# Causal scores cut into four blocks of 32 keys on four column strips, and a slab's TensorE work drawn together into one block

## The chip, the cores and the metric

The kernel runs on one core of a Trainium2 chip. The metric is device time in microseconds from the start to the end of one execution; 652.51 us is the median of three executions of the kernel before (652.41, 652.51 and 654.05). TensorE (PE) multiplies matrices; the loading of its stationary operand has its own rows (PEld). VectorE (DVE), ScalarE (ACT) and GpSimd (POOL) work elementwise, and SyncE (SP) issues the DMAs, in order.

## The reference

A gated linear attention over 768 steps for 4 batches of 8 heads of 48, and a feed-forward layer over its 3072 rows:

```python
def _attn_ref(q, k, v, a_re, a_im):
    mag = np.sqrt(a_re * a_re + a_im * a_im)
    scale = np.minimum(mag, 0.999) / (mag + 1e-06)
    a_re_n, a_im_n = a_re * scale, a_im * scale
    for t in range(S):
        ar, ai = a_re_n[:, :, t, :, None], a_im_n[:, :, t, :, None]
        new_re = ar * S_re - ai * S_im
        new_im = ar * S_im + ai * S_re
        kv = np.einsum('bhd,bhe->bhde', k[:, :, t], v[:, :, t])
        S_re, S_im = new_re + kv, new_im
        y[:, :, t] = np.einsum('bhd,bhde->bhe', q[:, :, t], S_re)
...
    g = x @ w_gate                                   # 384 x 1536
    return (g / (1.0 + np.exp(-g)) * (x @ w_val)) @ w_out
```

## The kernel before, in words

The sequence is cut into 6 chunks of 128 steps. A **slab** is one chunk of one batch (24 slabs, 0 to 23; slabs 0 to 3 are the first chunk, c = 0, and slabs 20 to 23 the last, c = 5). Two slabs form a group, and a group's 256 rows go through the feed-forward layer together (12 groups).

For a group, `stage_ops` turns decay and phase into scaled q and k of 96 columns per head (48 real, 48 imaginary; tiles `qs` and `ks`). `slab_ops` transposes them to 96 partitions (tile `T`) and then has TensorE do three things for a slab:

- **scores** (`sc0`, `sc1`, line 628, PSUM tile `p_ps`): for each of the 8 heads one f32 product of 128 keys by 128 queries over 96 rows, four heads in one operation; VectorE multiplies them with the causal mask (`mk0`, `mk1`, line 634, tile `sc`);
- **state and values** (`av`, line 659, tile `p_py`): the outputs lie in 12 blocks of 32 columns on four column strips of the array (partitions 0, 32, 64, 96 of PSUM), and each block adds the old state times q (`p_py<-T,G`, 96 rows, only where c > 0) and the masked scores times v (`p_py<-sc,vt`, 128 rows), in steps of four matmuls, one on each strip;
- **new state** (`kv`, line 686, tile `p_pm`): 24 products of 32 by 48 on three strips (not in the last chunk), which VectorE adds to G (`ga`) and decays (`gm`).

Then ScalarE copies `p_py` to `xh` (`evh`) and VectorE keeps the rest in `xl` (`evl`). `ffn_ops` works on them in 12 steps per group: `f1` (line 839; from group 1 on 18 products of 128 by 256), silu on ScalarE, `h2`, `hh` and `hl` (VectorE or ScalarE), `f2` (line 873; 6 products of 128 by 384). A f32 matmul has two matmul records in the trace, and an operation of this kind takes twice the records that the program shows. `weight_ops` and `split_ops` make the weights from 64-bit words on VectorE in the first part (lines 738 to 746); `range_ops` loads them again later and reduces them on VectorE (`flags<-wo`, line 791) for a check of their range.

The order on every engine is fixed at build time by `Planner.plan`. It takes an operation when its engine is free in the plan, the one with the lowest key among those that are ready; keys come from due times (`ta` of a slab from `anchor`, `key` of a feed-forward step), and each operation has a cost written by hand, such as `{"PE": 0.88}`. Constants at the top (SWITCH, STRETCH, T0, PER, ...) set due times and penalties. At run time every engine takes its instructions in that order, and waits on semaphores where an operand isn't there.

Of the kernel before, what the change touches and what calls it, by code (L numbers as in the profile page):

```python
# [33 lines left out]
SWITCH_KEY = 8.8  # L34
STRETCH = 1.749
AHEAD, YIELD, QUEUED = -15.32, 14.38, 5.384
T0, PER, FT, FT0 = 47.32, 23.02, 3.999, 5.679
LEAD0, LEAD2 = 8.605, 2.123
CONV0, CONVP = 39.06, 28.89
T1 = T0 + 12 * FT0  # L40
CK0, CKP = 167.9, 18.96
# [4 lines left out]
SHY = -9.417  # L46
# [9 lines left out]
class Op:  # L56
    def __init__(self, idx, name, engs, fn, deps, alloc, table, aim, lat, move, port):
        self.port = port
        self.idx, self.name, self.engs, self.fn, self.deps = idx, name, engs, fn, deps
        self.alloc, self.table, self.aim, self.lat, self.move = alloc, table, aim, lat, move  # L60
        self.start = self.end = self.eng = self.load = None


class Planner:
# [5 lines left out]
    def add(self, name, engs, fn, deps=(), alloc=(), use=(), table=None, key=None, lat=0.0, move=0.0,  # L70
# [7 lines left out]
        return name  # L78

# [15 lines left out]
    def plan(self):  # L95
# [9 lines left out]
        loads = []  # L105
        left, order = [op for op in self.ops if not missing[op]], []
        while left:
            ready = {e: [] for e in free}
            for op in left:
                t = max([d.end + HOP for d in op.deps], default=0.0)  # L110
# [84 lines left out]
def quick(ctx, tc, q, k, v, a_re, a_im, w_gate, w_val, w_out, out, count):  # L195
# [12 lines left out]
    mask = tri.bitcast(F32)  # L208
    ident = const.tile([P, P], F32, name="ident")
# [9 lines left out]
    vts = [const.tile([P, H, 64], F32, name=f"vt{i}") for i in range(2)]  # L219
# [34 lines left out]
    slots = dict(qs=1, ks=1, T=2, dec=3, sc=2, sg=2, hh=2, hl=2, ost=2, xh=2, xl=2, vt=2,  # L254
# [3 lines left out]
    PSUMS = ("gv", "po", "ps", "py", "pm")  # L258
# [13 lines left out]
    for t in fixed:  # L272
        slots[t] = 1
    pl = Planner(slots)
# [277 lines left out]
    def slab_ops(n):  # L552
# [61 lines left out]
        def ldv(e):  # L614
            at_["vt", n] = vts[n % 2]
            nc.sync.dma_start(out=vts[n % 2][:, :, 0:D], in_=v[b, c * P:c * P + P])
        pl.add("ldv" + N, {"SP": 0.55}, ldv, deps=[f"ldv{n - 1}"] if n else [], alloc=[("vt", n)], lat=1.4, move=1.09)
# [4 lines left out]

        for qd in range(2):
            def sc(e, qd=qd):
                qT, kT = views()
                ps = new("ps", f"{n}.{qd}").rearrange("p (h t) -> p h t", h=4)
                for hh in range(4):
                    nc.tensor.matmul(out=ps[:, hh, :], lhsT=kT(4 * qd + hh), rhs=qT(4 * qd + hh), start=True, stop=True)  # L628
            pl.add(f"sc{qd}_{n}", {"PE": 0.88}, sc, deps=tdeps + [f"sc0_{n}" if qd else f"sc1_{n - 1}"],
                   alloc=[("ps", f"{n}.{qd}")], use=[("T", n)], key=ta + qd)  # L630

            def mk(e, qd=qd):
                s = new("sc", f"{n}.{qd}")
                nc.vector.tensor_tensor(out=s, in0=at_["ps", f"{n}.{qd}"].rearrange("p (h t) -> p h t", h=4),  # L634
                                        in1=mask.unsqueeze(1).to_broadcast([P, 4, P]), op=ALU.mult)
            pl.add(f"mk{qd}_{n}", {"DVE": 0.6}, mk, deps=[f"sc{qd}_{n}"], alloc=[("sc", f"{n}.{qd}")],
                   use=[("ps", f"{n}.{qd}")])

        def av(e):
            qT, kT = views()  # L640
            py = new("py", n)[:, :DM].rearrange("p (k t) -> p k t", k=KT)
            vf, gf = flat(vts[n % 2]), flat(G[:, b])

            turns = [[] for _ in range(4)]
            for blk in range(12):
                pr, j = divmod(blk, 3)
                slot, kt_ = blk % 4, blk // 4
                o = py[32 * slot:32 * slot + 32, kt_, :]
                heads = ([(2 * pr, 128 * pr)], [(2 * pr, 128 * pr + 32), (2 * pr + 1, 128 * pr + 48)],
                         [(2 * pr + 1, 128 * pr + 80)])[j]  # L650
                mm = []
                for h, col in heads:
                    if c > 0:
                        mm.append((gf[:, col:col + 32], qT(h)))
                    mm.append((vf[:, col:col + 32], at_["sc", f"{n}.{h // 4}"][:, h % 4, :]))
                turns[slot] += [(o, l, r, i == 0, i == len(mm) - 1) for i, (l, r) in enumerate(mm)]
            for step in zip(*turns):
                for slot, (o, l, r, opens, closes) in enumerate(step):
                    nc.tensor.matmul(out=o, lhsT=l, rhs=r, start=opens, stop=closes, tile_position=(0, 32 * slot))  # L659
        pl.add("av" + N, {"PE": 2.2 if c else 1.3}, av, deps=[f"mk0_{n}", f"mk1_{n}", "ldv" + N, f"gm{n - 4}"],  # L660
               alloc=[("py", n)], use=[("sc", f"{n}.0"), ("sc", f"{n}.1"), ("T", n), ("vt", n)], key=ta + 5)

# [6 lines left out]
        pl.add("evh" + N, {"ACT": 0.4}, evh, deps=["av" + N] + ([f"evh{n - 1}"] if half else []),  # L669
# [10 lines left out]
        if c < NCH - 1:  # L680
            def kv(e):
                pk = new("pm", "K" + N)[:96, :HD].rearrange("p (h d) -> p h d", h=H)
                ks, vt = at_["ks", ("ks", g)][:, hs], vts[n % 2]
                for h in range(H):
                    for j in range(3):
                        nc.tensor.matmul(out=pk[32 * j:32 * j + 32, h, :], lhsT=ks[:, h, 32 * j:32 * j + 32],  # L686
# [438 lines left out]
```

## Time and profile before

| | before |
|---|---|
| median of three executions | 652.51 us |
| the profiled execution | 652.97 us |
| its span, first to last instruction | 651.3 us |
| PE busy | 619.1 us (95%) |
| DVE busy | 498.9 us (77%) |
| ACT busy | 397.5 us (61%) |
| POOL busy | 2.9 us |
| mean granted TensorE clock | 0.999 |

Times in the trace run from the start of the span. "Busy" is time in which at least one instruction of the engine ran; matmuls overlap in the pipeline, so that the distance from one start to the next tells more of a matmul's cost than its length does.

### The profile page before, as it was taken

The numbers are of one execution on the slowest core, as the hardware profiler recorded it, in microseconds if no ns is written. First come the engines' busy times: TensorE is split into PE (matmuls) and PEld (weight loads), VectorE is DVE, ScalarE is ACT, GpSimd is POOL, SyncE is SP. The second block draws the span as 40 slices with busy tenths as digits, with TensorE's granted clock in tenths as the row PEclk, the third lists the DMA queues.
The fourth block names the chain that finished last, engine by engine and source line by source line (L and its number), as shares of the span: only waits on it lengthen the run. The fifth ranks groups of instructions, "written<-read, shape, count | busy, mean of one in ns | idle before, by whom it ended". The sixth has DMA issues, their size and how long they took to land.

```text
span 651.3 us, 15505 instructions
## 1 busy us (share of the span) xinstructions
PE 619.1 (95%) x6306; PEld 578.3 (89%) x6306; DVE 498.9 (77%) x923; ACT 397.5 (61%) x654; POOL 2.9 (0%) x9
## 2 busy tenths in 40 slices
PE   2789999899999999999999999999999999999996
PEld 1467778899998999999999999999999999999995
DVE  8899999989877867977967976966966966643332
ACT  7955259876876958747947757967847836211111
POOL 1000000000000000000000000000000000000000
PEclk9999999999999999999999999999999999999999
DMA  7999102224635544654644555554542530320000
GB/s 233 314 279 361 40 26 74 60 88 124 173 99 148 151 123 115 180 118 118 188 111 118 163 131 123 146 127 119 129 105 60 127 90 16 76 51 1 25 1 29
DMA packets 141748, 77.49 MB, mean 119 GB/s; under 512 B 102363, under 2 KB 137437, under 8 KB 141670
## 3 DMA queue, kind: packets, MB, share of 16 engines
q1 hardware_dynamic: 141670, 76.43, 43.6%
q8 instruction: 51, 0.84, 0.6%
q14 instruction: 27, 0.22, 0.1%
HBM read 57.47 MB, written 4.78 MB: 96 GB/s over the span
## 4 chain that ended last, share of the span: by engine, by line
PE 64%; DVE 17%; ACT 7%; DMA 6%; issue 4%; SPq 1%; DVEq 0%; ACTq 0%
PE p_gv L839 33%; PE p_po L873 16%; PE p_py L659 5%; PE p_ps L628 5%; ACT L956 2%; ACT s L360 2%; DVE xl L742 2%; DMA wo<-in_moe_w_val_dram 2%; PE p_pm L686 2%; PE p_pm L455 2%; DMA wo<-in_moe_w_out_dram 1%; DMA re<-in_a_re_dram 1%; DVE sg L850 1%; DVE sc L634 1%; DVE s L305 1%
## 5 line engine op out<-in xcount | busy, mean ns | idle before, releaser
L839 PE MATMUL p_gv<-xh,ww 128*128 128x256 f32 x1596 | 311.3, 292 | 1.9 <-DVE sg L850 1.9
L839 PEld LDWEIGHTS p_gv<-xh,ww 128*128 128x128 f32 x1596 | 257.9, 190 | 10.7 <-DVE sg L850 4.1
L839 PE MATMUL p_gv<-xl,ww 128*128 128x256 f32 x726 | 202.9, 279 | 0.0
L956 ACT ACT_TABLE_LOAD x111 | 142.4, 1283 | 1.9
L839 PEld LDWEIGHTS p_gv<-xl,ww 128*128 128x128 f32 x726 | 136.4, 188 | 0.2 <-issue 0.2
L845 ACT ACTIVATE sg<-p_gv 128x256 f32<-128x256 f32 x144 | 53.7, 382 | 135.0 <-PE p_gv L839 134.2
L873 PE MATMUL p_po<-wo,hh 128*128 128x384 f32 x484 | 126.4, 342 | 0.0
L850 DVE TENSOR_TENSOR sg<-sg,p_gv 128x256 f32<-128x256 f32 x144 | 58.5, 413 | 61.0 <-ACT sg L845 60.9
L873 PEld LDWEIGHTS p_po<-wo,hh 128*128 128x128 f32 x484 | 81.2, 188 | 2.3 <-issue 2.0
L873 PE MATMUL p_po<-wo,hl 128*128 128x384 f32 x242 | 81.5, 337 | 0.0
L305 DVE TENSOR_TENSOR hl<-sg,hh 128x256 fp32r<-128x256 f32 x132 | 54.3, 417 | 6.7 <-ACT hh L309 1.5
L628 PE MATMUL p_ps<-T 96*128 96x128 f32 x384 | 53.2, 279 | 0.2 <-PE p_gv L839 0.2
L628 PEld LDWEIGHTS p_ps<-T 96*128 96x128 f32 x384 | 50.6, 196 | 1.3 <-PE p_gv L839 0.4
L873 PEld LDWEIGHTS p_po<-wo,hl 128*128 128x128 f32 x242 | 45.4, 188 | 0.0
L309 ACT CAST hh<-sg 128x256 fp32r<-128x256 f32 x49 | 19.8, 405 | 35.3 <-DVE sg L850 31.8
L360 ACT ACTIVATE s<-s 128x768 f32<-128x768 f32 x44 | 36.7, 842 | 5.4 <-DVE s L305 5.0
L659 PE MATMUL p_py<-sc,vt 128*32 128x128 f32 x768 | 37.3, 272 | 1.2 <-ACT xh L668 0.7
L791 DVE TENSOR_REDUCE flags<-wo 128x1 f32<-128x384 f32 x36 | 19.7, 547 | 24.2 <-DMA wo<-in_moe_w_val_dram 11.4
L634 DVE TENSOR_TENSOR sc<-p_ps,tri 128x512 f32<-128x512 f32 x48 | 32.7, 680 | 3.1 <-PE p_ps L628 2.7
L659 PE MATMUL p_py<-T,G 96*32 96x128 f32 x640 | 33.5, 280 | 0.0
L796 ACT ACTIVATE wo<-wo 128x384 f32<-128x384 f32 x36 | 20.1, 558 | 12.8 <-DMA wo<-in_moe_w_gate_dram 6.7
L311 DVE CAST hh<-sg 128x256 fp32r<-128x256 f32 x83 | 23.6, 288 | 4.2 <-PE p_po L873 0.4
(134 smaller groups left out, 804.0 us busy)
## 6 DMA issues: line engine op xcount, KB each, us to landing
T<-ww SPq DMA_DIRECT2D x216, 64.0 KB, 2.1
wo<-in_moe_w_out_dram SPq DMA_DIRECT2D x24, 384.0 KB, 6.6
ww<-in_moe_w_gate_dram SPq DMA_DIRECT2D x12, 384.0 KB, 5.2
vt<-in_v_dram SPq DMA_DIRECT2D x24, 192.0 KB, 3.8
ww<-in_moe_w_val_dram SPq DMA_DIRECT2D x12, 384.0 KB, 5.9
out_dram<-ost SPq DMA_DIRECT2D x24, 192.0 KB, 2.1
wo<-in_moe_w_gate_dram SPq DMA_DIRECT2D x12, 384.0 KB, 3.4
wo<-in_moe_w_val_dram SPq DMA_DIRECT2D x12, 384.0 KB, 3.9
```

What stands on the lines that cost most here:

```text
L305: V[e].tensor_tensor(out=out, in0=a, in1=b, op=op)
L311: nc.vector.tensor_copy(out=out, in_=in_)
L360: nc.scalar.activation(out=of(dst), in_=of(source), func=func, scale=scale, **kw)
L628: nc.tensor.matmul(out=ps[:, hh, :], lhsT=kT(4 * qd + hh), rhs=qT(4 * qd + hh), start=True, stop=True)
L634: nc.vector.tensor_tensor(out=s, in0=at_["ps", f"{n}.{qd}"].rearrange("p (h t) -> p h t", h=4), in1=mask.unsqueeze(1).to_broadcast([P, 4, ...
L659: nc.tensor.matmul(out=o, lhsT=l, rhs=r, start=opens, stop=closes, tile_position=(0, 32 * slot))
L796: nc.scalar.activation(out=high(0), in_=high(1), func=AF.Square, accum_out=flags[:, fl_hi + j:fl_hi + j + 1])
L839: nc.tensor.matmul(out=gv[:, i, :], lhsT=l, rhs=r, start=(m == 0), stop=(m == len(mm) - 1))
L845: nc.scalar.activation(out=new("sg", I), in_=at_["gv", I][:, 0:2 * P], func=AF.Silu)
L850: nc.vector.tensor_tensor(out=sg, in0=sg, in1=at_["gv", I][:, 2 * P:4 * P], op=ALU.mult)
L873: nc.tensor.matmul(out=po, lhsT=l[:, cs], rhs=weight("o", f, part), start=f == 0 and j == 0, stop=f == NF - 1 and j == len(products) - 1)
L956: nc.scalar.preload_act_table_set(op.load)
```

## The change: what it does

- A head's scores are no longer one product of 128 keys by 128 queries but four blocks of 32 keys. Block i has only the queries from 32 i on (128, 96, 64 and 32 columns), since earlier queries see none of its keys. Each block stands on one of the four column strips; strip (i + r) mod 4, where r is the head's place, so that every strip gets blocks of all lengths. The helper `strips` writes the matmuls in the order in which their strips come free by column count.
- Keys of a head are thereby rotated by 32 r partitions. The mask becomes a tile `turn` of 128 x 4 x 128, made at the start on GpSimd; v is loaded a second time with the same rotation (`ldr`, seven DMAs for a slab, tile `vr`), and the unrotated v (`ldv`, contiguous now) is left for `kv` alone, and isn't loaded in the last chunk. The score banks and `vr` are set to zero once at the start on VectorE.
- `av` is split into `st` (state times q, 16 matmuls) and `V` (scores times v, 16 matmuls), and `kv` moves ahead of both. For c > 0, `glue` makes the planner keep TensorE for the chain sc, kv, st, V once sc has begun: nothing else comes between. `sc` then waits for all that the chain needs (T, v, rotated v, `ks`, the decayed state, the banks of `p_py` and `p_pm`).
- `mk0` and `mk1` both follow the whole `sc`.
- 15 of the planner's constants have other numbers, so that other operations change places too.

```diff
-        for qd in range(2):
-            def sc(e, qd=qd):
-                qT, kT = views()
-                ps = new("ps", f"{n}.{qd}").rearrange("p (h t) -> p h t", h=4)
-                for hh in range(4):
-                    nc.tensor.matmul(out=ps[:, hh, :], lhsT=kT(4 * qd + hh), rhs=qT(4 * qd + hh), start=True, stop=True)
+        def strips(turns):
+            ends = [0] * 4
+            while any(turns):
+                slot = min((s for s in range(4) if turns[s]), key=lambda s: ends[s])
+                o, l, r, opens, closes = turns[slot].pop(0)
+                ends[slot] += r.shape[-1]
+                nc.tensor.matmul(out=o, lhsT=l, rhs=r, start=opens, stop=closes, tile_position=(0, 32 * slot),
+                                 skip_group_check=True)
+        def sc(e):
+            qT, kT = views()
+            turns = [[] for _ in range(4)]
+            for qd in range(2):
+                for r in range(4):
+                    h = 2 * r + qd
+                    for i in range(4):
+                        slot = (i + r) % 4
+                        turns[slot].append((scores[qd][32 * slot:32 * slot + 32, r, 32 * i:P], kT(h)[:, 32 * i:32 * i + 32],
+                                            qT(h)[:, 32 * i:P], True, True))
+            strips(turns)
...
+        def ldr(e):
+            for r in range(4):
+                for p, t, m in ((32 * r, 0, P - 32 * r), (0, P - 32 * r, 32 * r)):
+                    if m:
+                        nc.sync.dma_start(out=turned_v[n % 2][p:p + m, 2 * r:2 * r + 2, 0:D],
+                                          in_=v[b, c * P + t:c * P + t + m, 2 * r:2 * r + 2])
...
-        pl.add("av" + N, {"PE": 2.2 if c else 1.3}, av, deps=[f"mk0_{n}", f"mk1_{n}", "ldv" + N, f"gm{n - 4}"],
-            pl.add("kv" + N, {"PE": 1.1}, kv, deps=made["ks"] + ["ldv" + N, "av" + N], alloc=[("pm", "K" + N)],
+        link = ["sc" + N]
+        if c < NCH - 1:
+            link.append(pl.add("kv" + N, {"PE": 0.85}, kv, deps=made["ks"] + ["ldv" + N, "sc" + N], alloc=[] if together else kvs,
+        if c > 0:
+            link.append(pl.add("st" + N, {"PE": 0.9}, states, deps=["sc" + N, f"gm{n - 4}"] + ["kv" + N] * (c < NCH - 1),
+        link.append(pl.add("V" + N, {"PE": 1.0 if c else 1.2}, values, deps=[f"mk0_{n}", f"mk1_{n}", "ldr" + N] + ["st" + N] * (c > 0),
+        if together:
+            pl.glue(*link)
...
-        for t in vts:
+        for t in turned_v + scores:
             nc.vector.memset(t, 0.0)
```

The places on TensorE, from slab 8 (c = 2). Before, the scores stand on line 628 in two operations with feed-forward work (`p_gv`, `p_po`) between, and state and values alternate in steps of four on line 659:

```order
L628 MATMUL p_ps<-T 128x128 x4
L873 MATMUL p_po<-wo_929,hh 128x384 x2
...
L628 MATMUL p_ps<-T 128x128 x4
L839 MATMUL p_gv<-xh,ww_918 128x256
...
L659 MATMUL p_py<-T,G 32x128 x4
L659 MATMUL p_py<-sc,vt_79 32x128 x4
L659 MATMUL p_py<-T,G 32x128 x4
...
L873 MATMUL p_po<-wo_959,hh 128x384 x2
...
L686 MATMUL p_pm<-vt_79,ks 32x48 x24
```

After, the same slab is one run of 88 matmuls; the first and the last score blocks are shown (32 in all, of 128, 96, 64 and 32 columns), then new state, state and values:

```order
L656 MATMUL p_ps_90<-T 32x128
L656 MATMUL p_ps_90<-T 32x96
L656 MATMUL p_ps_90<-T 32x64
L656 MATMUL p_ps_90<-T 32x32
...
L656 MATMUL p_ps_91<-T 32x32
L716 MATMUL p_pm<-vt_72,ks 32x48 x24
L656 MATMUL p_py<-T,G 32x128 x16
L656 MATMUL p_py<-sc,vr_74 32x128 x16
L933 MATMUL p_po<-wo_1141,hh 128x384 x2
```

`kv` now stands between the scores and the rest, and no feed-forward work is left between the scores and the values that wait for `mk0` and `mk1`.

On VectorE, the same slab. Before, the two masks (`sc<-p_ps,tri`) stand with another operation between them:

```order
L599 STREAM_TRANSPOSE ww_1400<-ks 128x4x2x3x32
L599 STREAM_TRANSPOSE ww_1400<-qs 128x4x2x3x32
L634 TENSOR_TENSOR sc<-p_ps,tri 128x512
L424 SCALAR_TENSOR_TENSOR s_2413<-s_2413,s_2302 128x768
L634 TENSOR_TENSOR sc<-p_ps,tri 128x512
```

After, they stand one behind the other in every slab, here right behind a reduction of weights that come by DMA (`flags<-wo`) and behind products of the feed-forward steps (`sg`, `hh`, `hl`):

```order
L910 TENSOR_TENSOR sg<-sg,p_gv 128x256 x2
L324 CAST hh<-sg 128x256 x2
L318 TENSOR_TENSOR hl<-sg,hh 128x256 x2
L851 TENSOR_REDUCE flags<-wo_1472 128x1
L679 TENSOR_TENSOR sc<-p_ps_90,turn 128x512
L679 TENSOR_TENSOR sc<-p_ps_91,turn 128x512
L910 TENSOR_TENSOR sg<-sg,p_gv 128x256
L318 TENSOR_TENSOR G<-G,p_pm 96x8x48
```

What stands ahead of the masks differs from slab to slab.

## Rows read from the trace of the kernel before

**Rows 1.** The page: span, busy time of engines, and the first line of the chain that ended last.

```profile
span 651.3 us, 15505 instructions
PE 619.1 (95%) x6306; PEld 578.3 (89%) x6306; DVE 498.9 (77%) x923; ACT 397.5 (61%) x654; POOL 2.9 (0%) x9
...
PE 64%; DVE 17%; ACT 7%; DMA 6%; issue 4%; SPq 1%; DVEq 0%; ACTq 0%
```

**Rows 2.** Busy time by stretch: from and to, length, then busy us (and instructions) of PE, PEld, DVE, ACT, POOL, the granted clock, the DMA engines' share and GB/s.

```profile
30.00:60.00 30.00, 27.15 (x293) 22.41 (x291) 30.00 (x50) 18.80 (x28) 0.00 (x0) 1.00 1.02 308
60.00:90.00 30.00, 30.00 (x212) 23.91 (x211) 30.00 (x54) 8.79 (x16) 0.00 (x0) 1.00 0.26 87
90.00:105.00 15.00, 13.71 (x133) 10.19 (x132) 15.00 (x27) 11.99 (x16) 0.00 (x0) 1.00 0.16 40
105.00:130.00 25.00, 23.24 (x169) 21.48 (x168) 24.72 (x48) 21.85 (x36) 0.00 (x0) 1.00 0.28 79
130.00:160.00 30.00, 29.95 (x369) 28.74 (x370) 27.24 (x44) 21.35 (x34) 0.00 (x0) 1.00 0.37 105
160.00:600.00 440.00, 435.81 (x4773) 420.20 (x4773) 330.10 (x621) 283.53 (x468) 0.00 (x0) 1.00 0.46 116
600.00:640.00 40.00, 40.00 (x304) 40.00 (x303) 14.75 (x39) 5.78 (x15) 0.00 (x0) 1.00 0.03 11
```

**Rows 3.** Timeline of PE around state, values and new state of one slab: start, length of the merged piece, what, and how many records.

```profile
287.63 0.28 PE L839 MATMUL p_gv<-xh,ww 128*128 128x256 f32 x1
287.83 0.43 PE L659 MATMUL p_py<-T,G 96*32 96x128 f32 x8
288.09 0.40 PE L659 MATMUL p_py<-sc,vt 128*32 128x128 f32 x8
288.31 0.41 PE L659 MATMUL p_py<-T,G 96*32 96x128 f32 x8
...
289.45 0.40 PE L659 MATMUL p_py<-sc,vt 128*32 128x128 f32 x8
289.78 0.62 PE L873 MATMUL p_po<-wo,hh 128*128 128x384 f32 x2
290.24 0.34 PE L873 MATMUL p_po<-wo,hl 128*128 128x384 f32 x1
290.42 0.51 PE L873 MATMUL p_po<-wo,hh 128*128 128x384 f32 x2
290.76 0.34 PE L873 MATMUL p_po<-wo,hl 128*128 128x384 f32 x1
291.03 0.88 PE L686 MATMUL p_pm<-vt,ks 128*32 128x48 f32 x48
291.84 0.38 PE L839 MATMUL p_gv<-xh,ww 128*128 128x256 f32 x1
292.06 0.28 PE L839 MATMUL p_gv<-xl,ww 128*128 128x256 f32 x1
292.18 0.40 PE L839 MATMUL p_gv<-xh,ww 128*128 128x256 f32 x2
```

**Rows 4.** Timeline of PE around the scores, from three slabs, and one place (35.19) where the values waited for the mask.

```profile
35.19 0.85 PE L659 MATMUL p_py<-sc,vt 128*32 128x128 f32 x20 [0.26 <-DVE sc L634]
...
282.63 0.28 PE L839 MATMUL p_gv<-xh,ww 128*128 128x256 f32 x1
282.75 1.10 PE L628 MATMUL p_ps<-T 96*128 96x128 f32 x8
283.61 0.60 PE L873 MATMUL p_po<-wo,hh 128*128 128x384 f32 x2
284.05 0.34 PE L873 MATMUL p_po<-wo,hl 128*128 128x384 f32 x1
...
301.90 1.10 PE L628 MATMUL p_ps<-T 96*128 96x128 f32 x8
...
395.45 1.10 PE L628 MATMUL p_ps<-T 96*128 96x128 f32 x8
```

**Rows 5.** Timeline of DVE at the masks of three slabs: the brackets give how long the engine had sat idle, and for whom.

```profile
34.45 0.68 DVE L634 TENSOR_TENSOR sc<-p_ps,tri 128x512 f32<-128x512 f32 x1
35.06 0.55 DVE L738 TENSOR_SCALAR xl<-ww 128x768 uint32<-128x768 uint32 x1
...
303.04 0.69 DVE L634 TENSOR_TENSOR sc<-p_ps,tri 128x512 f32<-128x512 f32 x1 [0.33 <-PE p_ps L628]
...
396.66 0.56 DVE L791 TENSOR_REDUCE flags<-wo 128x1 f32<-128x384 f32 x1 [4.08 <-DMA wo<-in_moe_w_val_dram]
397.13 0.95 DVE L305 TENSOR_TENSOR s<-im,s 128x768 fp32r<-128x768 f32 x1
397.99 0.41 DVE L850 TENSOR_TENSOR sg<-sg,p_gv 128x256 f32<-128x256 f32 x1
398.32 0.68 DVE L634 TENSOR_TENSOR sc<-p_ps,tri 128x512 f32<-128x512 f32 x1
```

**Rows 6.** Who waited for whom over the whole span: us in total, times, longest.

```profile
DVE sg L850 <- ACT sg L845: 60.9, 43, 1.9
...
DVE flags L791 <- DMA wo<-in_moe_w_val_dram: 11.4, 5, 4.1
DVE flags L791 <- DMA wo<-in_moe_w_gate_dram: 10.0, 5, 4.2
...
PE p_py L659 <- DVE sc L634: 0.5, 2, 0.3
```

**Rows 7.** Timeline of SP's queue: one load of v.

```profile
21.36 0.62 SPq L616 DMA_DIRECT2D vt<-in_v_dram  x1
```

**Rows 8.** Timeline of DVE at the start.

```profile
1.70 1.03 DVE L926 MEMSET vt<- 128x512 f32 x2
3.26 2.55 DVE L372 RECIPROCAL ww<-ww 128x384 f32<-128x384 f32 x1 [0.54 <-DMA ww<-in_a_re_dram]
```

**Rows 9.** Timeline of POOL at the start.

```profile
1.98 0.29 POOL L921 TENSOR_SCALAR_AFFINE_SELECT ident<-ident 128x128 f32<-128x128 f32 x1
2.21 1.80 POOL L927 MEMSET G<- 96x2048 f32 x1
```

More of the change, by code (lines that the diff above doesn't have):

```diff
@@ L60, in __init__ @@
         self.alloc, self.table, self.aim, self.lat, self.move = alloc, table, aim, lat, move
[L61 removed]
+        self.start = self.end = self.eng = self.load = self.next = None
 class Planner:
@@ L273, in quick @@
         slots[t] = 1
+    scores = [psum.tile([P, 4, P], F32, name=f"p_ps{i}", tag=f"ps{i}", bufs=1) for i in range(2)]
     pl = Planner(slots)
@@ L636, in slab_ops @@
[L636 to L644, printed above, removed]
+                nc.vector.tensor_tensor(out=s, in0=scores[qd], in1=turn, op=ALU.mult)
+            pl.add(f"mk{qd}_{n}", {"DVE": 0.6}, mk, deps=["sc" + N], alloc=[("sc", f"{n}.{qd}")],
+                   use=[("ps", f"{n}.{qd}")], key=ta + 3)
@@ L656, in av @@
[L656 to L659, printed above, removed]
-        pl.add("av" + N, {"PE": 2.2 if c else 1.3}, av, deps=[f"mk0_{n}", f"mk1_{n}", "ldv" + N, f"gm{n - 4}"],
-               alloc=[("py", n)], use=[("sc", f"{n}.0"), ("sc", f"{n}.1"), ("T", n), ("vt", n)], key=ta + 5)
+                yield slot, kt_, py[32 * slot:32 * slot + 32, kt_, :], heads
@@ new lines, in states, with values @@
+        def states(e):
+            qT, kT = views()
+            new("py", n)
+            turns, gf = [[] for _ in range(4)], flat(G[:, b])
+            for slot, kt_, o, heads in blocks():
+                turns[slot] += [(o, gf[:, col:col + 32], qT(h), kt_ == 0 and i == 0, False) for i, (h, col) in enumerate(heads)]
+            strips(turns)
+        def values(e):
+            if c == 0:
+                new("py", n)
+            turns, vf = [[] for _ in range(4)], flat(turned_v[n % 2])
+            for slot, kt_, o, heads in blocks():
+                for i, (h, col) in enumerate(heads):
+                    m, r = place_of(h)
+                    turns[slot].append((o, vf[:, col:col + 32], at_["sc", f"{n}.{m}"][:, r, :], c == 0 and i == 0, i == len(heads) - 1))
+            strips(turns)
@@ new lines, in kv @@
+        def kv(e):
+            pk = new("pm", "K" + N)[:96, :HD].rearrange("p (h d) -> p h d", h=H)
+            ks, vt = at_["ks", ("ks", g)][:, hs], vts[n % 2]
+            for h in range(H):
+                for j in range(3):
+                    nc.tensor.matmul(out=pk[32 * j:32 * j + 32, h, :], lhsT=ks[:, h, 32 * j:32 * j + 32],
+                                     rhs=vt[:, h], start=True, stop=True, tile_position=(0, 32 * j))
+        sources = [("sc", f"{n}.0"), ("sc", f"{n}.1"), ("vr", n)]
```

84 lines of the change are left out of this document (48 added, 36 removed).

## The prediction

> **What bounds the kernel now.** I read the page first: TensorE is busy for 619.1 of 651.3 us, and the chain that ended last runs on it for 64% [rows 1]. The table by stretch then tells two parts apart [rows 2]. From 30 to 105 us VectorE has no idle time at all (30.00 of 30.00 twice, 15.00 of 15.00), and up to 130 us nearly none; it converts weights there, and TensorE still has gaps. From 130 us on TensorE has none to speak of (435.81 of 440.00 us between 160 and 600) while VectorE works for 330.10 of these 440. So what is taken from TensorE before about 130 us is worth little, and behind it nearly all. By the order of the program, slabs 0 to 3 lie in the first part and slabs 4 to 23 in the second. The granted clock is 1.00 in every stretch, the upper of the two levels, so that no part of the sum is at the other.
>
> **What a slab costs TensorE now.** I count what a slab takes out of the feed-forward stream, from start to start, and with it the slower start of what follows.
>
> - Scores: from 282.75 to 283.61 is 0.86 us. The feed-forward piece behind it has 0.44 us from its first to its third matmul (283.61 to 284.05) where 0.34 is usual (290.42 to 290.76), so 0.10 more: 0.96 us, twice per slab, 1.92 us [rows 3, 4].
> - State and values: after the matmul at 287.63 the next was due 0.12 us later, the usual distance (292.06 to 292.18); it came at 287.83, 0.08 late. Eight steps up to 289.78 are 1.95 us, and the start behind it is slow by 0.12 (289.78 to 290.24 against 0.34). Together 2.15 us [rows 3].
> - New state: due at 290.94 (0.18 after 290.76, as 290.24 to 290.42), begun at 291.03: 0.09; 0.81 us up to 291.84; then 0.22 to 292.06 where 0.12 is usual, 0.10 more. Together 1.00 us [rows 3].
>
> Sum: 5.07 us, and 4.07 without the new state in the last chunk.
>
> **What it costs afterwards.** The price of a step on four strips is seen at the state and values: four f32 matmuls of 128 columns take 0.22 to 0.23 us from start to start (288.09 to 288.31, and 1.62 us for seven steps), about 0.225 [rows 3]. The strips run at the same time, for one such matmul at full width takes 0.86/4 = 0.215 us alone [rows 4]. A head's four blocks have 128 + 96 + 64 + 32 = 320 columns; eight heads on four strips make 640 columns per strip, five steps: 1.13 us instead of 1.92. The bounds of this are the bare column count (640/1024 of 1.72 us, 1.08) and the rate at which the new state's narrow matmuls pass, 48 in 0.88 us or 0.018 each [rows 3], which gives 64 x 0.018 = 1.17. I take 1.13. The new state keeps its 0.81 us less one change of layout, 0.72. State and values become four steps each, 0.90 us each, and alternate no more. There is one entrance (0.08) and one exit (from 289.45 + 0.225 to 289.78 is 0.10, and 0.12 of slow start: 0.22). Sum: 0.08 + 1.13 + 0.72 + 0.90 + 0.90 + 0.22 = 3.95 us, and a wait w that is new.
>
> **The new wait.** Values need both masks, and nothing but new state and state (0.72 + 0.90 = 1.62 us) lies between them and the scores; before, feed-forward steps lay there. The least that the masks need: the scores' results are out about 0.18 us after the next step could begin (a step lasts 0.40 us and the next starts after 0.22 [rows 3]); the mask starts 0.04 us behind that (303.00 to 303.04 [rows 4, 5]); the second follows after 0.61 us (34.45 to 35.06 [rows 5]) and lasts 0.68; TensorE begins 0.06 us later (35.13 to 35.19 [rows 4, 5]). Together 1.57 us: covered, with 0.05 us to spare. But this holds only if VectorE is free when the scores end. Between 160 and 600 us it is busy for 75% of the time with instructions of 0.53 us in the mean (330.10/621) [rows 2], so an instruction under way costs 0.75 x 0.27 = 0.20 us on average, and up to 0.95. The engine takes its instructions in order, and so one that itself waits holds the masks too: products that wait for ScalarE (43 times, 60.9 us), reductions that wait for a DMA (10 times, 21.4 us) [rows 6]. Before, this cost nothing: the mask at 398.32 started 1.77 us after its scores were out at 396.55, behind a reduction that had waited 4.08 us [rows 4, 5]. In the new order such a reduction stands right ahead of the masks in slab 8. I add 0.20 us for these and take w = 0.4; the bounds are 0 and 1.77. Behind the waiting values on TensorE the whole feed-forward stream is queued.
>
> **The sum.** Slabs 4 to 19 (c = 1 to 4): 5.07 - 3.95 - 0.4 = 0.72 us each, 11.5 us. Slabs 20 to 23 have no new state to cover the masks: 3.23 us of work, 1.57 - 0.90 = 0.67 of bare wait, 0.4 more: 4.30 against 4.07, a loss of 0.9 us for the four. Slab 7 stands one f2 ahead of its group's first f1, which needs its output by way of ScalarE and VectorE; a wait of some 0.4 us is to be expected. Slabs 0 to 3: nothing, since VectorE sets the pace there and its work stays the same but for small things. Net 10.2 us: 652.97 - 10.2 = 642.8 for an execution like the profiled one; the median lies 0.5 us lower, **642.5 us** with rounding. For any other w the gain is 18.2 - 20 w (16 x 1.12 + 4 x 0.17 - 0.4, and w once in each of 20 slabs).
>
> **Edits costed at nothing.** Two more memsets on VectorE, 0.5 us each, fall where it waits 0.54 us for the first load [rows 8]; 0.5 us at most are left, in a stretch where later waits take them up. The mask tile on GpSimd needs a memset and seven selections like the one of 0.29 us, and G's memset of 1.80 us moves behind them [rows 9]; the masks use it near 34 us [rows 5]. Seven more loads per slab take SP 7 x 0.62 = 4.3 us [rows 7], of the 22 us that a slab has (440 us for some 20 slabs, [rows 2]); what is queued behind them are the transposed tiles' and the weights' loads. They are issued one to two slabs ahead, as the tiles alternate. If the cover failed, the reductions would wait longer and w with them, which is inside its bounds; from 30 to 60 us the DMA engines are full (share 1.02 [rows 2]), and a delay of a few us there is the price.
>
> **The rivals.**
>
> 1. *The masks come late as a rule.* VectorE's in-order wait for a DMA or for ScalarE falls ahead of the masks in most slabs. It decides from w = 0.91 on, where 18.2 - 20 w is nothing; at w = 1.1 it is a loss of 3.8 us, 656 us: slower. For it speaks the mask at 398.32, against it that at 303.04, where VectorE itself had idled 0.33 us [rows 5]. Chance 0.09. With w between 0.65 and 0.8 the gain is 5.2 to 2.2 us, 647 to 650; chance 0.13.
> 2. *Narrow matmuls don't get cheaper.* If every matmul record had a least time of its own, whatever its columns, the 64 records of the scores could not pass faster than that allows. The nearest rows on both sides are the new state, 0.018 us per record of 48 columns, and the steps of state and values, 8 records in 0.225 or 0.028 us per record of 128 columns [rows 3]. At 0.028 the scores would take 1.80 us, 0.67 more than in my sum, over 20 slabs 13 us: 656 us, slower. The 48-column row is against it, since it passes below that; only the 32-column blocks are narrower than anything in the trace. Here a page speaks against the change: the Trainium skill, "TensorE: Matmul & The Clock Gate", section "Wait — 56ns, not 53.3ns?", says that start-to-start of matmuls never drops below about 25 ns, however few columns they have. By that rule 48 records of the new state would take an estimated 1.2 us; the trace shows 0.88, so it doesn't hold across strips. Chance 0.04.
> 3. *More is gained.* If w is near 0 in most slabs, the gain comes to 15 to 18 us; and slab 3 and its neighbours, in a stretch that has TensorE busy for 30.00 of 30.00 [rows 2], may give something too: 633 to 637 us. Chance 0.12.
>
> The forecast's own case, w between 0.15 and 0.65, has 0.62 and gives 637 to 647.
>
> **How the numbers follow.** About 0.3%, 2 us, is what a measurement of this kernel can tell from no change. Faster by more (under 650.5): 0.62 + 0.12 and most of the milder late case (0.10), together 0.84. Within 2 us: the rest of that case and the near end of the late one, 0.05. Slower: 0.11. The range from 635 to 651 us leaves out the two slow rivals and the far end of the third.
>
> **What would show it.** The new block should stand in the timeline as one piece of about 4.0 us, with the scores at 1.1 to 1.2 and no gap but one, ahead of the values, of 0.4 us in the mean and released by VectorE's mask line. TensorE's waits for that line, 0.5 us in all before [rows 6], should come to 6 to 11 us, most evenly in the last four slabs. VectorE should be without idle time up to about 105 us as before, and the first step of group 1 should begin within 2 us of where it did. Wrong would be: scores over 1.4 us; gaps ahead of the block (for T, v or a bank) where I have none; a first part longer by more than 3 us.

## The result, and the profile after

The changed kernel takes 657.03 us (median of four, 657.02 to 657.18) against 652.53 us for the kernel before on the same chip: a ratio of 1.0064, 95% interval 1.0047 to 1.0081. It is slower by 0.6%, where 1.5% faster was forecast. The page of its profiled execution:

```profile
span 655.3 us, 18071 instructions
PE 609.7 (93%) x7458; PEld 566.2 (86%) x7458; DVE 504.9 (77%) x938; ACT 399.8 (61%) x648; POOL 6.4 (1%) x17
...
PE 58%; DVE 19%; DMA 9%; SPq 5%; ACT 4%; issue 4%; POOL 0%; DVEq 0%; ACTq 0%; POOLq 0%
```

Against [rows 1], TensorE is busy for 9.4 us less, and yet the span is 4.0 us longer: the time went into waits. In the chain that ended last, TensorE fell from 64 to 58%, DMA rose from 6 to 9% and SP's queue from 1 to 5%. By stretch (columns as in [rows 2]):

```profile
30.00:60.00 30.00, 23.74 (x424) 18.95 (x425) 26.66 (x44) 13.15 (x23) 0.00 (x0) 0.94 0.85 252
60.00:90.00 30.00, 27.75 (x198) 20.61 (x199) 26.61 (x49) 14.15 (x20) 0.00 (x0) 0.94 0.66 220
90.00:105.00 15.00, 15.00 (x192) 11.96 (x182) 14.55 (x25) 7.53 (x11) 0.00 (x0) 1.00 0.34 55
105.00:130.00 25.00, 24.60 (x169) 22.60 (x168) 25.00 (x51) 22.17 (x35) 0.00 (x0) 1.00 0.20 48
130.00:160.00 30.00, 28.09 (x499) 25.72 (x498) 28.21 (x47) 21.36 (x32) 0.00 (x0) 1.00 0.41 117
160.00:600.00 440.00, 428.29 (x5607) 412.23 (x5607) 338.79 (x634) 289.54 (x471) 0.00 (x0) 1.00 0.49 123
```

VectorE, which had no idle time from 30 to 90 us, has 6.7 us of it, and the DMA engines' share fell from 1.02 to 0.85. The granted clock is 0.94 on average in these two stretches: it is at its lower level from 45.4 to 48.8 us and from 72.7 to 76.1, and at the upper one in the rest. As marks I take the first silu of group 1 (106.31 us before, 111.13 after) and the last silu of all (641.62, 645.22). So **the first part lost 4.8 us, and behind it only 1.2 us were gained**, where 0 and 10.2 were forecast.

The block itself is as forecast. Slab 11 on TensorE:

```profile
309.04 0.28 PE L899 MATMUL p_gv<-xh,ww 128*128 128x256 f32 x1
309.25 1.40 PE L656 MATMUL p_ps<-T 96*32 96x128 f32 x64
310.47 0.82 PE L716 MATMUL p_pm<-vt,ks 128*32 128x48 f32 x45
...
311.15 1.11 PE L656 MATMUL p_py<-T,G 96*32 96x128 f32 x31
312.05 1.09 PE L656 MATMUL p_py<-sc,vr 128*32 128x128 f32 x32
313.07 0.61 PE L933 MATMUL p_po<-wo,hh 128*128 128x384 f32 x2
313.52 0.33 PE L933 MATMUL p_po<-wo,hl 128*128 128x384 f32 x1
```

Scores take 1.22 us from start to start (309.25 to 310.47), new state 0.63 (its matmuls mix with the state's first at 311.10), state 0.95, values 1.02. From the start of the matmul ahead of the block to the start behind it are 4.03 us. Slabs 11 and 17 are this short; a block without new state would take 4.03 - 0.63 = 3.40. The 20 blocks of slabs 4 to 23 sum to 93.2 us where 16 x 4.03 + 4 x 3.40 = 78.1 are work: a wait of 0.75 us each. Part of it stands ahead of the values, for the masks, and part has no releaser:

```profile
PE p_py L656 <- issue: 7.1, 7, 3.3
...
DVE flags L851 <- DMA wo<-in_moe_w_gate_dram: 4.9, 4, 3.2
PE p_py L656 <- DVE sc L679: 3.8, 9, 1.6
DVE flags L851 <- DMA wo<-in_moe_w_val_dram: 2.4, 1, 2.4
```

These are the waits over the whole span, as in [rows 6]. Of the 7.1 us without a releaser, 3.3 are one wait of slab 1 in the first part, where the values begin right behind a late mask (the second mask ends at 43.48, the values start at 43.59). The idle times are shorter than what a wait costs, since the matmuls under way still drain in its beginning.

### The profile page after: what moved, and what is told of

It is laid out like the page before. It is cut to its first block, busy times and chain, and to the rows that moved or that the text cites. A ratio compares the mean times of both kernels' runs of the same rounds, so it can differ in the third digit from the quotient of the medians.

```text
span 655.3 us, 18071 instructions
## 1 busy us (share of the span) xinstructions
PE 609.7 (93%) x7458; PEld 566.2 (86%) x7458; DVE 504.9 (77%) x938; ACT 399.8 (61%) x648; POOL 6.4 (1%) x17
## 4 chain that ended last, share of the span: by engine, by line
PE 58%; DVE 19%; DMA 9%; SPq 5%; ACT 4%; issue 4%; POOL 0%; DVEq 0%; ACTq 0%; POOLq 0%
PE p_gv L899 31%; PE p_po L933 16%; PE p_py L656 5%; PE p_ps L656 3%; SPq L621 3%; DMA wo<-in_moe_w_out_dram 2%; DMA wo<-in_moe_w_gate_dram 2%; ACT L1023 2%; DVE sg L910 2%; DVE ww L318 1%; DVE s L318 1%; PE p_pm L716 1%; DVE sc L679 1%; SPq L789 1%; SPq L637 1%
## 5 line engine op out<-in xcount | busy, mean ns | idle before, releaser
L933 PEld LDWEIGHTS p_po<-wo,hl 128*128 128x128 f32 x242 | 45.4, 188 | 0.9 <-DVE hl L318 0.9
L656 PE MATMUL p_py<-sc,vr 128*32 128x128 f32 x768 | 32.1, 275 | 10.9 <-issue 6.8
L656 PEld LDWEIGHTS p_py<-sc,vr 128*32 128x32 f32 x768 | 23.6, 109 | 16.4 <-DVE sc L679 7.7
L656 PEld LDWEIGHTS p_ps<-T 96*32 96x32 f32 x1536 | 30.8, 110 | 6.6 <-ACT T L322 2.5
L656 PE MATMUL p_ps<-T 96*32 96x96 f32 (+3 forms) x1536 | 34.1, 239 | 1.5 <-ACT T L322 1.5
L851 DVE TENSOR_REDUCE flags<-wo 128x1 f32<-128x384 f32 x36 | 19.7, 547 | 18.2 <-DMA wo<-in_moe_w_out_dram 10.8
L679 DVE TENSOR_TENSOR sc<-p_ps,turn 128x512 f32<-128x512 f32 x48 | 30.7, 679 | 1.4 <-PE p_ps L656 1.2
L737 ACT CAST xh<-p_py 128x384 fp32r<-128x384 f32 x22 | 10.5, 476 | 33.7 <-PE p_py L656 33.6
L322 ACT CAST hh<-sg 128x256 fp32r<-128x256 f32 x43 | 17.4, 405 | 20.1 <-DVE sg L910 18.2
```

What stands on the lines that cost most here:

```text
L679: nc.vector.tensor_tensor(out=s, in0=scores[qd], in1=turn, op=ALU.mult)
L851: nc.vector.tensor_reduce(out=flags[:, fl_lo + j:fl_lo + j + 1], in_=high(1), axis=AX.X, op=ALU.min, apply_absolute_value=True)
L933: nc.tensor.matmul(out=po, lhsT=l[:, cs], rhs=weight("o", f, part), start=f == 0 and j == 0, stop=f == NF - 1 and j == len(products) - 1)
```

## The experiments

**Theory A:** SP's queue. The seven loads of rotated v for a slab take SP's time, and what is queued behind them (inputs of the stages, weights, transposed tiles) comes late, in the first part and later; VectorE and ScalarE then wait, in order, and the masks behind them. **Rivals:** the new order of operations; the transfers themselves (short packets); the wait for the masks in the block; the gaps without a releaser. Each run was timed beside the kernel before on its own chip (652.49 us for the first four, 654.08 for the next, 653.36 for the last), so that ratios are what to compare; the changed kernel has 1.0064.

### Who is late in the first part, and in slab 21

Read from the changed kernel's trace, SP's queue first, then ScalarE and VectorE (in brackets the idle time and its releaser):

```profile
42.92 4.38 SPq L637 DMA_DIRECT2D vr<-in_v_dram  x7
...
52.59 5.28 SPq L637 DMA_DIRECT2D vr<-in_v_dram  x7
...
60.09 0.71 SPq L365 DMA_DIRECT2D re<-in_a_re_dram  x1
...
67.23 0.84 ACT L393 ACTIVATE s<-re 128x768 f32<-128x768 f32 x1 [4.28 <-DMA re<-in_a_re_dram]
...
41.93 0.96 DVE L318 TENSOR_TENSOR qs<-qt,s 128x768 f32<-128x768 f32 x1 [2.55 <-DMA dr<-qs]
...
71.96 0.42 DVE L910 TENSOR_TENSOR sg<-sg,p_gv 128x256 f32<-128x256 f32 x1 [2.94 <-ACT sg L905]
```

The load of `re` for group 2 goes out at 60.09 now. ScalarE stands 4.28 us for it, the silu behind it is late, and VectorE stands 2.94 us for the silu. The same load in the kernel before, in e2 (the seven loads on GpSimd's queue) and in e8 (one load instead of seven), both below:

```profile
46.21 0.84 SPq L352 DMA_DIRECT2D re<-in_a_re_dram  x1
...
52.39 0.40 SPq L365 DMA_DIRECT2D re<-in_a_re_dram  x1
...
55.06 0.48 SPq L365 DMA_DIRECT2D re<-in_a_re_dram  x1
```

So of the 13.9 us between before and after, 5 to 8 are the loads; the rest is there without them too, and goes with the new order of operations. Slab 21 shows the same in the second part: SP, VectorE, TensorE of the changed kernel,

```profile
529.53 1.90 SPq L621 DMA_DIRECT2D T<-ww  x3
531.52 4.52 SPq L637 DMA_DIRECT2D vr<-in_v_dram  x7
536.10 5.89 SPq L621 DMA_DIRECT2D T<-ww  x9
542.10 0.53 SPq L847 DMA_DIRECT2D wo<-in_moe_w_out_dram  x1
...
545.21 0.55 DVE L851 TENSOR_REDUCE flags<-wo 128x1 f32<-128x384 f32 x1 [1.97 <-DMA wo<-in_moe_w_out_dram]
...
547.05 1.28 DVE L679 TENSOR_TENSOR sc<-p_ps,turn 128x512 f32<-128x512 f32 x2
...
545.06 1.11 PE L656 MATMUL p_py<-T,G 96*32 96x128 f32 x32
547.79 0.41 PE L656 MATMUL p_py<-sc,vr 128*32 128x128 f32 x4 [1.61 <-DVE sc L679]
```

and the same slab with the loads on GpSimd's queue (run e2 below):

```profile
518.41 8.25 SPq L621 DMA_DIRECT2D T<-ww  x12
526.77 0.53 SPq L847 DMA_DIRECT2D wo<-in_moe_w_out_dram  x1
...
532.07 0.55 DVE L851 TENSOR_REDUCE flags<-wo 128x1 f32<-128x384 f32 x1
...
534.15 1.28 DVE L679 TENSOR_TENSOR sc<-p_ps,turn 128x512 f32<-128x512 f32 x2
...
533.98 1.13 PE L656 MATMUL p_py<-T,G 96*32 96x128 f32 x32
534.90 0.41 PE L656 MATMUL p_py<-sc,vr 128*32 128x128 f32 x4
```

Seven loads of 4.52 us stand in the middle of the transposed tile's. The weights' load behind both goes out at 542.10, the reduction waits 1.97 us for it, the masks stand behind the reduction, and TensorE waits for them with the feed-forward stream behind. With the seven loads off this queue, neither the reduction's 1.97 us nor TensorE's 1.61 us is there (a wait of 0.17 us for the second mask is left).

### e2 and e8: the loads off SP's queue, and one load instead of seven

```diff
-                        nc.sync.dma_start(out=turned_v[n % 2][p:p + m, 2 * r:2 * r + 2, 0:D],
+                        nc.gpsimd.dma_start(out=turned_v[n % 2][p:p + m, 2 * r:2 * r + 2, 0:D],
```

> The changed kernel with the seven loads of rotated v issued by GpSimd's queue instead of SP's, in all slabs; same loads, same order elsewhere. Theory A, SP's queue: first silu of group 1 near 107 us, 652 to 653 us, and the waits for weights and transposed tiles later on are shorter too. Rival C, the transfers themselves (many short packets on full DMA engines): the first part stays as long, 656 to 657 us, whatever the run without these loads in the first chunk gives.

Measured: 644.12 us, ratio 0.9880 (0.9856 to 0.9905). This version is faster than both kernels, and by more than theory A expected. From the first silu of group 1 to the last it needs 523.1 us instead of the changed kernel's 534.1: 11.0 us, with the same transfers and the same order. In the first part little is won: the first silu of group 1 comes at 109.52, 1.6 us earlier than in the changed kernel and still 3.2 later than before. VectorE waits there,

```profile
42.67 0.96 DVE L318 TENSOR_TENSOR qs<-qt,s 128x768 f32<-128x768 f32 x1 [3.18 <-DMA dr<-qs]
...
52.91 0.42 DVE L910 TENSOR_TENSOR sg<-sg,p_gv 128x256 f32<-128x256 f32 x1 [2.34 <-ACT sg L905]
```

while the DMA engines are full (share 1.01 from 30 to 45 us and 1.03 from 45 to 60). So rival C, the transfers, falls for the second part and stays open for the first.

```diff
         def ldr(e):
-            for r in range(4):
...
+            nc.sync.dma_start(out=turned_v[n % 2][:, :, 0:D], in_=v[b, c * P:c * P + P])
```

> The changed kernel with one load of v in place of seven in all slabs, on SP's queue at the same place, with the same waits for the buffer (the rotation is left out, so the values are those of the wrong keys). Theory A1, the issue time of the loads (0.5 to 0.6 us each, 86 us in all): as with GpSimd's queue, 643 to 646. Theory A2, SP stands waiting for the buffer of rotated v that the values two slabs ago give back, and holds what is behind it: then the time stays at 653 or more, since the wait is the same with one load.

Measured: 643.35 us, 0.9837 (0.9819 to 0.9854). So it is not the wait for the buffer, since the one load waits at the same place; behind the first silu of group 1 it needs 523.3 us, as e2 does, and there it is the issue time. The first part is back as well, which e2's was not. In the stretches of this run,

```profile
30.00:60.00 30.00, 25.39 (x476) 20.02 (x477) 28.64 (x47) 13.78 (x24) 0.00 (x0) 1.00 0.99 311
60.00:90.00 30.00, 29.72 (x295) 23.42 (x290) 29.71 (x55) 15.21 (x21) 0.00 (x0) 1.00 0.46 159
...
160.00:600.00 440.00, 435.72 (x5686) 422.44 (x5685) 339.93 (x644) 287.25 (x470) 0.00 (x0) 1.00 0.47 121
```

VectorE has 1.65 us of idle time from 30 to 90 us instead of 6.7, the DMA engines are full again from 30 to 60 us, and TensorE has back what it had in [rows 2] from 160 us on. The first silu of group 1 comes at 106.02 us, the last silu at 629.36. Rows of all the loads of rotated v (instructions; ns of one as least, median, most), SP in the changed kernel and GpSimd in e2:

```profile
L637 SPq DMA_DIRECT2D vr<-in_v_dram x168: 315/484/1751, 4.9 to 552.4; - x168
...
L637 POOL DMA_DIRECT2D vr<-in_v_dram x168: 542/611/1373, 7.7 to 539.9; - x168
```

GpSimd takes longer for each (0.611 against 0.484 us in the median), but nothing stands behind them there. The Trainium skill, "DMA: Bandwidth & Descriptors", section "Rules for kernel authors", says that spreading DMAs over issuing engines gives no bandwidth and only saves the sequencer issue time; the runs agree that it saves issue time (in e2 the same bytes move), and behind the first part that time was the cost.

### e1 and e5: only the first chunk's loads

```diff
+            if c == 0:
+                nc.sync.dma_start(out=turned_v[n % 2][:, :, 0:D], in_=v[b, c * P:c * P + P])
+                return
...
-                        slot = (i + r) % 4
+                        slot = (i + r) % 4 if c else i
...
```

> The changed kernel, but in the first chunk (slabs 0 to 3) keys are not rotated and v comes in one load instead of seven; the order on every engine stays that of the changed kernel. Theory A, SP's queue: the seven loads of a slab take 4.4 to 5.3 us of SP's queue, four times before 58 us, and push the stage and weight loads behind them (the last weight load is issued at 67.17 us, 59.40 in the kernel before). Then the last weight load goes out near 61 us, VectorE's waits at 39.4 (2.55 us) and 69.0 (2.94 us) go, the first silu of group 1 comes near 107 instead of 111.1 us, and the time is about 653 us. Rival B, the other order of operations: it stays at 656 to 657 with the first silu of group 1 at 111. The scores of slabs 0 to 3 get about 0.6 us longer each (1024 columns on the fullest strip instead of 640).

Measured: 657.92 us, 1.0086 (1.0068 to 1.0103): a miss. In the profiled execution the first silu of group 1 does come at 107.39, but that execution was the shortest of five (654.22, the others 657.03 to 659.16), and from there to the last silu it needs 535.6 us, not less than the 534.1 of the changed kernel. Theory A in the form "the first chunk's loads cost 4 us" doesn't hold by itself; the loads of all slabs count. Where the other executions lost the first part's gain isn't known. The same edit with all loads on GpSimd's queue:

> The changed kernel with rotated v loaded by GpSimd's queue in all slabs, and in the first chunk unrotated keys with v in one load. Theory: the first part still lost 3.2 us with GpSimd issuing (VectorE waits 3.18 us from 39.5 us on for a small round trip through DRAM behind full DMA engines, 2.34 us from 50.6); with 24 loads fewer before 58 us these waits shrink, the first silu of group 1 comes near 107 us instead of 109.5, and the time is 641 to 643 instead of 644.1. Rival: these waits come from the order of operations alone; then it stays at 644.

Measured: 644.52 us, 0.9862 (0.9837 to 0.9888), not to be told from e2, as the rival has it. In its trace the first silu of group 1 comes at 108.00 instead of 109.52; a gain of 1.5 us in the first part of one trace is too little for the times to show.

### e7 and e11: the seven loads in the kernel before

```diff
+    more_v = [const.tile([P, H, 64], F32, name=f"vr{i}") for i in range(2)]
...
             nc.sync.dma_start(out=vts[n % 2][:, :, 0:D], in_=v[b, c * P:c * P + P])
+            for r in range(4):
+                for p, t, m in ((32 * r, 0, P - 32 * r), (0, P - 32 * r, 32 * r)):
+                    if m:
+                        nc.sync.dma_start(out=more_v[n % 2][p:p + m, 2 * r:2 * r + 2, 0:D],
+                                          in_=v[b, c * P + t:c * P + t + m, 2 * r:2 * r + 2])
```

> The kernel before, with nothing of the change but the loads: beside each load of v seven more on SP's queue, into tiles that nobody reads (24 x 7; one load of v per slab stays). Theory A, SP's queue: it gets slower by as much as GpSimd's issuing gave back in the changed kernel, 13 us: 660 to 667; at least 5 us. Rival D: the loads hurt only where masks and values wait for each other in one block; then it stays within 2 us of 652.5.

Measured: 699.14 us, 1.0694 (1.0647 to 1.0740), 45 us slower, far more than expected. Two of its waits; in [rows 6] the same two are 11.4 and 10.0 us:

```profile
DVE flags L797 <- DMA wo<-in_moe_w_val_dram: 28.9, 7, 8.3
...
DVE flags L797 <- DMA wo<-in_moe_w_gate_dram: 16.9, 4, 7.8
```

In this execution the granted clock is at its lower level for 34 us between 43 and 491 us; what share of the 45 us that has wasn't separated. In e11 the planner is told (`{"SP": 4.4}` in place of 0.55 for this operation):

> The kernel before with the seven loads of e7 (699.14 us), but the planner told of them: the cost of the load of v on SP is 4.4 instead of 0.55, so that all engines' orders are planned anew around it. Theory: seven loads that are planned for cost what they cost in the changed kernel, where the plan knows them, some 10 to 15 us: 662 to 672. Rival: the number planned doesn't matter, SP's time does: 690 or more.

Measured: 665.46 us, 1.0187 (1.0174 to 1.0201), 12.1 us slower, as expected. So the loads hurt a kernel without strips, block or glue too (e7). With a plan that knows of them it loses about as much as the changed kernel did, a quarter of what it loses without; but e11's order is another one throughout, and a new order can cost or save as much by itself (e12), so that the 12.1 us are not shown to be the price of the loads alone.

### e9: four loads

```diff
-                for p, t, m in ((32 * r, 0, P - 32 * r), (0, P - 32 * r, 32 * r)):
+                for p, t, m in ((32 * r, 0, P - 32 * r),):
```

> The changed kernel with four of the seven loads per slab, on SP's queue (the three that wrap around are left out, so part of the values is missing). One load per slab gave 643.35 us, seven 657.03. If each load costs in proportion, four give 643.35 + 13.7 x 3/6 = 650. If the queue has slack that is used up only near seven, 643 to 646; if the cost comes with the first few already, 655 to 658.

Measured: 647.34 us, 0.9906 (0.9888 to 0.9925), between the first two cases. By ratios, times 652.5: from one load to four 4.5 us, from four to seven 10.3. The price grows faster than the number. (The four also move only five eighths of the bytes.)

### e3 and e10: values that don't wait for the masks

```diff
-                    turns[slot].append((o, vf[:, col:col + 32], at_["sc", f"{n}.{m}"][:, r, :], c == 0 and i == 0, i == len(heads) - 1))
+                    turns[slot].append((o, vf[:, col:col + 32], turn[:, r, :], c == 0 and i == 0, i == len(heads) - 1))
```

> The changed kernel, but the values step multiplies the constant mask tile instead of the masked scores (that part of the result is left out), so that TensorE no longer waits for the masks; VectorE still makes them, and all orders stay. Theory: in slabs 4 to 23 the masks cost 8.4 us of the 15 us by which the blocks exceed 4.03 us (3.40 in the last chunk), and 3.5 us more in slab 1; so about 647 to 649 us, and the gaps without a releaser in the middle of a block (slabs 4, 6, 8, 10, 16, 18; 5 to 6 us together) stay. Rival: the gaps ahead of the values are the arrival of instructions too; then less than 3 us is gained.

Measured: 659.86 us, 1.0120 (1.0099 to 1.0141): no gain, a loss of some 3 us. In its trace the loss lies in the first part (first silu of group 1 at 114.08 instead of 111.13), and from there to the last silu it needs 533.7 us against 534.1. The theory's 8 to 10 us are not there, and the rival's reason is not the right one either. TensorE's waits from 111 us on:

```profile
PE p_gv L899 <- DVE sg L910: 5.0, 9, 1.3
PE p_py L656 <- issue: 4.4, 6, 1.7
```

The line for the masks is gone, but that for VectorE's products went from 2.4 to 5.0 us. Values (busy time and the idle time ahead of them) took 34.7 us from the first silu of group 1 on and take 28.0, 6.8 us less; the idle time ahead of f1, f2 and the scores grew by 6.7. TensorE now waits a little later for engines that are as late as before. With SP's queue free it is otherwise:

> The kernel with GpSimd's queue for rotated v (644.1 us), and values that multiply the constant mask tile instead of the masked scores, as in the run without the wait for the masks (659.86 on the changed kernel, no gain). Theory: with the loads off SP's queue TensorE is the bound behind 130 us, so that now the wait for the masks is worth what the blocks show, about 3.5 us in slabs 4 to 23 and up to 3 in slab 1: 638 to 642. Rival: VectorE is the bound in its place; 644 or more.

Measured: 641.16 us, 0.9807 (0.9786 to 0.9827): 3.0 us less than e2 by the medians, 4.8 by the ratios. In the two traces 2.2 us of it lie ahead of the first silu of group 1 and 1.3 behind. So the wait for the masks had a price with SP's queue free, and none that the times show with the loads on it.

### e4 and e6: the gaps without a releaser

In slab 10 of the changed kernel the values stop for 1.09 us, with two records to go:

```profile
286.10 1.24 PE L656 MATMUL p_py<-sc,vr 128*32 128x128 f32 x30
288.43 0.38 PE L656 MATMUL p_py<-sc,vr 128*32 128x128 f32 x2 [1.09 <-issue]
```

Counted through all of TensorE's instructions in the trace (weight loads, matmuls, semaphores), the six gaps of this kind in slabs 4, 6, 8, 10, 16 and 18 (0.85, 1.27, 0.50, 1.37, 0.94 and 0.42 us from start to start) begin at numbers that are all 193 modulo 256. TensorE's instructions come by DMA in packets of 16 KB, 60 of them on the page (the trace has 15,059 instructions of TensorE, 59 times 256):

```profile
q8 instruction: 60, 0.98, 0.7%
```

The six gaps end 1.2 to 1.5 us after such a packet has been moved. A block is 88 f32 matmuls, 352 instructions in 4 us; of feed-forward pieces, 352 last over 20.

```diff
         nc.gpsimd.memset(G, 0.0)
+        for _ in range(24):
+            nc.tensor.matmul(out=scores[0][0:32, 0, 0:32], lhsT=ident[:, 32:64], rhs=ident[:, 0:32], start=True, stop=True)
```

> The changed kernel with 24 small f32 matmuls, 96 instructions of TensorE, ahead of all else at the start, where TensorE is idle. Theory P, arrival of instructions: the gaps without a releaser inside blocks fall on every 256th instruction of TensorE (all six at a count of 193 modulo 256), where the block has used up the instructions before the next 256 are there. Then the gaps move: the count stays 193 modulo 256, slabs 4, 6, 8 and 16 lose theirs (0.85, 1.27, 0.50, 0.94 us), slabs 5 and 19 get one of 0.5 to 1.3 us, slabs 15 and 21 perhaps a small one, 10 and 18 keep one; in sum some 4 instead of 6 us, 654 to 656 us. Rival Q, a wait for a load, a bank or a mask: the same slabs keep the gaps at the same matmul, and the time stays 657.

Measured: 660.05 us, 1.0131 (1.0107 to 1.0155). The mechanism is as theory P says: the number stays 193 modulo 256, slabs 4, 6, 8, 16 and 18 have no gap, and two of 0.30 and 0.34 us are left, in slabs 10 and 1 (fewer than expected). But the time does not follow, it is longer: as in e3, other waits grew (for VectorE's products 5.8 us instead of 2.4, for the masks 5.1 instead of 3.8). On the kernel of e5:

> As the run before (GpSimd issues, one load in the first chunk), and 96 instructions of TensorE ahead of all else, as in the shift by 96. Theory: with SP's queue free TensorE is the bound again behind 130 us, and then the gaps at every 256th instruction (2.9 us in the run with GpSimd alone) cost time: 2 to 3 us less than without the shift, 638 to 641. Rival: they are given back elsewhere as in the shift on the changed kernel (660.05 against 657): no gain, or a loss.

Measured: 644.92 us, 0.9853 (0.9831 to 0.9874), the same as e5. The gaps moved to slabs 11, 13, 15, 17 and 21 (the last, 0.41 us, stands behind the fourth record of the values, where e5 waits for the second mask, and may be that), but their sum is 2.5 us against 3.2 in e5, so this run could not price them. The Trainium skill, "Runtime: NRT & Kernel Launch", section "Instruction fetch mechanics", has the 256 instructions and calls the cost of crossing mostly hidden; the first agrees, and so does the second for most crossings, but not for the six of the changed kernel in blocks of narrow matmuls (up to 1.4 us each).

### e12: a plan that knows of GpSimd's queue

```diff
-                        nc.sync.dma_start(out=turned_v[n % 2][p:p + m, 2 * r:2 * r + 2, 0:D],
+                        nc.gpsimd.dma_start(out=turned_v[n % 2][p:p + m, 2 * r:2 * r + 2, 0:D],
...
-        pl.add("ldr" + N, {"SP": 3.85}, ldr, ...
+        pl.add("ldr" + N, {"POOL": 3.85}, ldr, ...
```

> The changed kernel with the loads of rotated v on GpSimd's queue, and the planner told so (their cost stands on GpSimd instead of SP, and the order is planned anew). If the 3.2 us that the first part still loses come from an order planned around a slow SP, 639 to 642; if a new order with constants chosen for another one is as good as any, 642 to 648.

Measured: 659.33 us, 1.0092 (1.0071 to 1.0112): outside both cases, 14 to 15 us slower than e2 with the same loads on the same queue. TensorE's idle time behind the first silu of group 1 is 19.6 us instead of 6.9, and 10.4 of it lie ahead of f1 and f2, for VectorE's products. So a new order has a price of its own, which can be as large as the change; which of its places costs most was not looked into.

## Why the prediction was wrong

- **Seven more loads at nothing: the step that failed.** It set 4.3 us of issue time against 22 us of a slab, as if the queue were empty, and bounded the price by "a few us" in the first part. The queue had its own work: all of SP's DMA rows behind the first silu of group 1 and up to 560 us sum to 198.6 us of 454 before, and 263.8 of 449 after. Even so it is not full; what is late is late behind unbroken rows of issues, as in slab 21, from 529.53 to 542.63. In the first part the 28 loads of slabs 0 to 3 hold it for 4.8, 4.4, 4.4 and 5.3 us ahead of 58 us, among the weights. The price is 14.8 us by the ratios of the changed kernel and e8, 12.0 by e2; by the traces of the changed kernel and e8, 5.1 of it lie ahead of the first silu of group 1 and 10.8 behind.
- **The first part at nothing:** 4.8 us lost, against "within 2 us"; the prediction's own sign of being wrong, a first part longer by more than 3 us, came true. With one load it was -0.3 (e8), with the seven on GpSimd's queue still 3.2 (e2), so that here issue time and transfers are not told apart. The lower level of the clock follows idle times of TensorE (3.35 us up to 43.59, for slab 1's masks, and 1.98 up to 72.44); in e8 the clock is 1.00. What share of the 4.8 us it has wasn't separated.
- **The wait w = 0.4:** 0.75 in the changed kernel, and the rival with w between 0.65 and 0.8 gave 647 to 650 us for that; the first part's 4.8 us and slightly dearer work make it a loss. Without the seven loads on SP's queue the same sum of blocks is 84.7 us (e8) and 85.8 (e2): w is 0.33 and 0.38. The forecast's w was that of a free queue. It came out for partly wrong reasons: the first mask doesn't wait for the whole scores (it starts 0.90 us after the scores' start, where the scores last 1.22, if VectorE is free), and the second is done 2.19 us after the scores' start, where the values could begin after 2.80, so that the cover is 0.6 us and not 0.05; for the same reason the bare wait of 0.67 us in slabs 20 to 23 isn't there (slabs 22 and 23 take 3.46 and 3.51 us in the changed kernel, against 4.30 in the forecast); and some 2 of the 6.6 us of wait in e8's blocks (5.4 of 15.1 in the changed kernel's) are gaps in the arrival of instructions, which the forecast did not have.
- **The work of a block:** 0.09 + 1.22 + 0.63 + 0.95 + 1.02 + 0.11 = 4.02 us by the forecast's own way of counting, against 3.95. Right.
- **Rival 2, a least time for narrow matmuls:** fell. The 64 records of the scores pass in 1.22 us, 0.019 each, where the forecast had 1.13 and the rival 1.80. The Trainium skill, "TensorE: Matmul & The Clock Gate", section "Wait — 56ns, not 53.3ns?", has 25 ns from start to start as the least; across strips that doesn't hold here.
- **Rival 1, late masks** by VectorE's in-order waits, was what the second part showed, but not as the rule of the block: its source was the queue of SP. TensorE's waits for the masks came to 3.8 us where 6 to 11 were forecast. The prediction had the chain itself ("If the cover failed, the reductions would wait longer and w with them"), left it inside the bounds of w, and gave it nothing in the sum.
- The sum without the cost of the loads is about what was measured: e8 is 10.6 us faster than before by its ratio, 12.3 by the spans of the two traces, where 10.2 were forecast. Part of that is luck, since w came out for partly wrong reasons.

## What to carry to other kernels

A queue that issues in order has a budget like an engine: before adding DMAs to it, sum the lengths of what it issues in that stretch, find the places where it issues without a break, and look at who waits for the loads behind. Splitting one load into seven for the sake of a layout cost more here (14.8 us) than the layout saved (10.6), and moving the seven to an idle queue gave most of it back (12.0). While a late supplier sets the pace, taking waits away elsewhere showed nothing here (e3, e4), so the supplier is to be tested first.

## What the runs showed of the hardware

- TensorE can run out of instructions: among dense narrow f32 matmuls there are gaps of 0.3 to 1.9 us without a releaser in the traces of these runs, each at an instruction whose number is 193 modulo 256, and they stay at that number when the program is shifted by 96 (e4). Only some of the blocks have one, 6 of 20 in the changed kernel; what decides it, and what such a gap costs, isn't shown.
- Matmuls of 32 to 128 columns on four strips start 0.019 us apart on average, with their weight loads.
- A DMA of 48 KB and less on SP's queue takes 0.48 us to issue in the median and up to 1.75; on GpSimd's 0.61, and up to 1.37.
